# Row remainders of two batches stored in one transfer, and the last output tile stored in two column halves

## The chip, the cores and the metric

The kernel runs on one core of one Trainium2 chip. The metric is the device time of one execution in microseconds. Three runs of the kernel before the change took 370.40, 368.73 and 370.27 us, so their median is 370.27 us.

## The reference

Eight batches of twelve heads go through attention whose denominator has one extra term, and the result, laid side by side by head as rows of 768 numbers, goes through a gated long convolution along the 448 positions of a batch and a last projection:

```python
scores = scale * np.matmul(q, k.transpose(0, 1, 3, 2))
m = np.max(scores, axis=-1, keepdims=True)
e = np.exp(scores - m)
attn = e / (np.sum(e, axis=-1, keepdims=True) + np.exp(-m) + 1e-09)
x = np.matmul(attn, v)                      # then heads side by side: B, S, 768
x1, x2, x3 = split(x @ w_proj, 3)           # each B, S, 768
x2_conv = irfft(rfft(x2, axis=1) * rfft(filter_fft, axis=0), axis=1)
return (x1 * x2_conv * x3) @ w_out          # out: 8, 448, 768, float32
```

The inputs q, k and v are 8 x 12 x 448 x 64, and the output is 8 x 448 x 768 in float32.

## The kernel before

Every piece of work is a task with an engine, a cost, tokens that it needs and makes, and buffers that it takes and gives back (`add`, L82). A planner (`Plan.run`, L90) walks the tasks in the order of a table, `plan.ORDER` (L433), with one number for each task, and writes each engine's instructions in the order that it finds. So the order is fixed when the program is built. Each engine works through its own list in order, and an instruction that waits holds up everything behind it on its engine.

Attention is worked by pairs of heads, six pairs to a batch and 48 in all. For the later batches SP (SyncE) loads q, k and v, POOL (GpSimd) casts them, and SP issues transposing transfers into `qT` (L628) and `kT` (L635) before TensorE makes the scores (L867, L869). The dense part of a batch follows: folds of the rows, a projection (L1096), for batches 3 to 7 a transposing transfer of that projection (L1113, tile `x2`, called `x` in the profile) and then the spectrum on TensorE (L1145), gates (L1197), the inverse transform and the gated product.

The output projection (`output`, L1009 and L1010) makes tiles of 128 rows and 384 columns in PSUM. A batch has 448 rows, that is three tiles of 128 rows (`st` 0 to 2) and a rest of 64. The rests of an even batch and of the odd one behind it share one tile (`st` 3 of the odd batch): partitions 0 to 63 hold the even batch's rest, 64 to 127 the odd one's. ScalarE copies each PSUM tile to half of the columns of an `osb` tile of 128 x 768 floats (`project_back`, L1319); three such buffers rotate. When both column halves (`ch` 0 and 1) are there, SP stores the tile (`store`): with one transfer for `st` 0 to 2 (L1326), with two for the shared rest tile, one to each batch (L1328 and L1329). So each row stored is 3,072 bytes long.

The last batch's tasks marked `keep` are written out at the very end, behind a branch to a slower, numerically safe version that is not taken here (L1540 is the tail behind it). There the tiles come in the order `st` 0, 1, 3, 2; three of the eight projections are made before the branch.

Of the kernel before, what the change touches and what calls it, by code (L numbers as in the profile page):

```python
# [18 lines left out]
B, H, S, DH = 8, 12, 448, 64  # L19
D = H * DH  # L20
SP = 112
# [4 lines left out]
DCH = 384  # L26
# [4 lines left out]
REM = S - 3 * 128  # L31
# [10 lines left out]
class Plan:  # L42
# [39 lines left out]
    def add(self, eng, cost, want, emit, need=(), make=(), take=(), give=(), dma=0.0, run=256, n=1, after=0.0, begun=(), late=0.0, turn=False, part=None, keep=False, port=False, rows=128):  # L82
        want = self.ORDER[len(self.tasks)] if self.ORDER else want + self.SHIFT.get(part, 0.0)
        if eng == "SP":
            dma *= self.STRETCH
        if eng == "DVE" and port:
            cost += self.SHARED
        self.tasks.append((want, len(self.tasks), eng, cost, emit, need, make, take, give, dma, after, run, n, begun, late, turn, keep, port or eng == "POOL" and not dma, rows))
# [227 lines left out]
def kernel(  # L316
# [11 lines left out]
    nc = tc.nc  # L328
# [105 lines left out]
    add = plan.add  # L434
# [583 lines left out]
    def dense(b, calm=True):  # L1018

        L = {}  # L1020
# [37 lines left out]
        for ds in (slice(0, 3), slice(3, 6)) if b else (slice(0, 3), slice(3, 4), slice(4, 6)):  # L1058
            g, m = ds.start, (ds.stop - ds.start) / 3
            slow = 0.3 + 0.7 * m  # L1060
            w = DENSE[b] - 2.5 - (0.4 if g else FOLD[b]) if b else FOLD0[(g + 1) // 2]
# [253 lines left out]
        def project_back(st, ch):  # L1315
            n = 128 if st < 3 or b % 2 else REM
            if ("os", st) not in L:
                L["os", st] = otp.tile([128, D], F32, name="osb")
            nc.scalar.copy(  # L1319
                L["os", st][:n, ch * DCH : (ch + 1) * DCH], L["O", st, ch][:n, :DCH]  # L1320
            )

        def store(st):
            osb = L["os", st]
            if st < 3:
                nc.sync.dma_start(out[b, st * 128 : (st + 1) * 128, :], osb)  # L1326
                return
            for i in range(1 + b % 2):  # L1328
                nc.sync.dma_start(out[b - b % 2 + i, 384:S, :], osb[i * REM : (i + 1) * REM])  # L1329

        def O(st, ch):
            keep = b + 1 == n_batches
            last = keep and (st, ch) not in TAIL
            hy, os_ = ("ho" if last else "hy", ("O", b, st, ch)), ("os", (b, st))
            if keep and not last:
                plan.open.append((st, ch))
            w = span(0.97, OUT[b])
            need = [("y", b, 0)] if st < 3 else [("y", b - b % 2, 1), ("y", b, 1)]
            mem_ = ("yT", b) if st < 3 else ("yR", b // 2)
            if 2 * st + ch < 3:  # L1340

                add("PE", 0.65, w, lambda: project(st, ch, 0, hy), need=[("y", b, 0, 0), ("y", b, 0, 1), "wout", ("G", b)],
                    make=[("O4", b, st, ch)], take=[hy])
                add("PE", 0.33, w + 1.5, lambda: project(st, ch, 1, hy), need=[("y", b, 0, 2), ("O4", b, st, ch)],
                    make=[("O", b, st, ch)], give=[mem_], keep=last)
            else:
                add("PE", 0.98, w, lambda: project(st, ch, None, hy), need=need + ["wout"], make=[("O", b, st, ch)],
                    take=[hy], give=[mem_], keep=last)
            add("ACT", 0.38, w, lambda: project_back(st, ch), need=[("O", b, st, ch)], make=[("os", b, st)],
                take=[os_], give=[hy], keep=keep)  # L1350
            if ch == 1:
                add("SP", 0.62, w, lambda: store(st), need=[("os", b, st)], make=[("store", b, st)], give=[os_], dma=0.87 if st < 3 else 1.1, run=180, keep=keep)
# [239 lines left out]
```

## Time and profile before

| | |
|---|---|
| median of three runs | 370.27 us (368.73 to 370.40) |
| time of the profiled execution | 369.05 us |
| its span, first to last instruction | 367.3 us |
| time around the span | 1.75 us |
| ScalarE copies of L1319 | 56, of 489 ns |
| stores of whole tiles (L1326) | 24, 384 KB each, landing 3.6 us after issue (median) |
| stores of rests (L1329) | 8, 192 KB each, landing 3.5 us after issue (median) |
| moved by DMA | 68.41 MB in 132,019 packets |

PE is TensorE, PEld its weight loads, DVE is VectorE, ACT is ScalarE, and a "q" behind an engine's name (SPq) marks its sequencer, which issues transfers. The DMA share is the mean busy share of the core's 16 DMA engines; it can read a little over 1, since packets of several transfers overlap. "Landing" is the time from the start of a transfer's issue to the signal that all its data has arrived.

### The profile page before, as it was taken

What the parts mean: (1) busy time and instruction counts of PE and PEld (TensorE: products, weight loads), DVE (VectorE), ACT (ScalarE), POOL (GpSimd) and SP (SyncE); (2) the same over time, 40 slices, a digit from 0 to 9 for tenths busy, and PEclk for the clock granted to TensorE, in tenths of its full rate; (3) what the DMA queues carried; (4) which work ended last, traced back from release to release, by engine and by line L of the source; (5) the groups of instructions that cost most, each with busy time, mean ns of one, the idle gap of its engine ahead of it and who ended that gap; (6) DMA issues with size and microseconds to landing.
All of it is one profiled execution on the core that took longest, in us unless ns stands there. A gap on an engine that the chain in (4) does not pass through costs nothing. (4 is left out here: it accounts for less than half of the span.)

```text
span 367.3 us, 9351 instructions
## 1 busy us (share of the span) xinstructions
PE 358.3 (98%) x3612; PEld 215.1 (59%) x3612; DVE 259.6 (71%) x671; ACT 262.0 (71%) x453; POOL 112.0 (30%) x247
## 2 busy tenths in 40 slices
PE   7999999999999999999999999999999999999995
PEld 6666665656655665654564555665555556565653
DVE  6678297984998587882787767783478848767570
ACT  5987886768777868876787766888688794464523
POOL 7680563243551444515226343321200000000000
PEclk9999999999999999999999999999999999999999
DMA  8999999979998999898999999899942066163125
GB/s 206 277 240 222 251 214 216 216 168 220 192 235 225 237 283 244 214 230 206 212 219 233 283 188 217 217 215 236 219 83 45 2 87 130 43 102 114 44 93 173
DMA packets 132019, 68.41 MB, mean 186 GB/s; under 512 B 88765, under 2 KB 128384, under 8 KB 131968
## 3 DMA queue, kind: packets, MB, share of 16 engines
q1 hardware_dynamic: 127248, 62.11, 75.1%
q0 software_dynamic: 4480, 5.41, 8.6%
q8 instruction: 29, 0.48, 0.5%
q10 hardware_dynamic: 240, 0.23, 0.3%
q14 instruction: 22, 0.18, 0.2%
HBM read 43.86 MB, written 11.01 MB: 149 GB/s over the span
## 5 line engine op out<-in xcount | busy, mean ns | idle before, releaser
L880 ACT ACTIVATE e<-psum 128x896 bf16<-128x896 f32 x138 | 122.1, 922 | 27.2 <-PE psum L867 25.5
L1197 PE MATMUL psum<-xT,wproj_bf 128*128 128x448 bf16 x576 | 121.6, 352 | 0.6 <-ACT cr L1253 0.6
L1197 PEld LDWEIGHTS <-wproj_bf 128*128 128x128 bf16 x576 | 53.9, 98 | 48.7 <-issue 5.4
L1010 PE MATMUL psum<-wout_bf,yT 128*128 128x384 bf16 x288 | 53.8, 326 | 0.0
L906 PE MATMUL psum<-vn,e 128*128 128x65 bf16 x1104 | 44.3, 194 | 0.0
L906 PEld LDWEIGHTS <-e 128*128 128x128 bf16 x1104 | 39.4, 98 | 6.5 <-issue 2.8
L867 PE MATMUL psum<-qT,kT 64*128 64x448 bf16 x288 | 42.1, 354 | 0.1
L1157 ACT CAST xs<-psum 113x384 bf16<-113x384 f32 (+1 forms) x64 | 29.2, 486 | 17.2 <-PE psum L1145 10.4
L664 POOL CAST nat<-nat 112x512 bf16<-112x512 f32 x36 | 23.5, 661 | 58.8 <-DMA nat<-in_q_dram 58.6
L1319 ACT COPY osb<-psum 128x384 f32<-128x384 f32 x56 | 25.7, 489 | 18.5 <-PE psum L1010 11.7
L1010 PEld LDWEIGHTS <-yT 128*128 128x128 bf16 x288 | 27.4, 98 | 18.0 <-issue 0.6
L1163 DVE TENSOR_TENSOR t<-xs,hrs 113x768 bf16<-113x768 bf16 (+1 forms) x64 | 36.5, 594 | 1.7 <-ACT xs L1157 1.6
L1096 PE MATMUL psum<-xf,wproj_bf 128*128 128x456 bf16 x180 | 37.5, 356 | 0.0
L921 DVE TENSOR_TENSOR xb<-psum,den 128x512 bf16<-128x512 f32 x48 | 33.2, 691 | 1.7
L1213 DVE TENSOR_TENSOR g<-x,psum 128x448 bf16<-128x448 bf16 x42 | 25.8, 616 | 10.2 <-PE psum L1197 7.5
L1253 ACT CAST cr<-psum 128x452 bf16<-128x452 f32 x48 | 24.7, 549 | 8.4 <-PE psum L1244 7.0
L1211 ACT CAST x<-psum 128x448 bf16<-128x448 f32 x42 | 22.3, 541 | 10.9 <-PE psum L1197 10.5
L684 POOL CAST nat<-nat 128x384 bf16<-128x384 f32 x29 | 16.3, 569 | 39.6 <-DMA nat<-in_k_dram 35.6
L886 ACT ACTIVATE er<-psum 128x448 bf16<-128x448 f32 x46 | 25.2, 557 | 4.2 <-PE psum L869 4.2
L1074 PE MATMUL psum<-wproj_bf,xf 128*113 128x384 bf16 x144 | 27.1, 328 | 0.0
L1096 PEld LDWEIGHTS <-wproj_bf 128*128 128x128 bf16 x180 | 17.0, 98 | 16.3 <-issue 1.5
L696 POOL CAST vn<-nat 128x192 bf16<-128x192 f32 x58 | 21.5, 401 | 16.2 <-DMA nat<-in_v_dram 15.6
(136 smaller groups left out, 477.1 us busy)
## 6 DMA issues: line engine op xcount, KB each, us to landing
nat<-in_q_dram SPq DMA_DIRECT2D x47, 224.0 KB, 4.4
out_dram<-osb SPq DMA_DIRECT2D x24, 384.0 KB, 3.6
nat<-in_k_dram SPq DMA_DIRECT2D x41, 192.0 KB, 4.8
nat<-in_v_dram SPq DMA_DIRECT2D x41, 192.0 KB, 4.5
wproj_bf<-in_moe_w_proj_dram POOLq DMA_DIRECT2D x2, 1152.0 KB, 12.2
rests<-in_k_dram SPq DMA_DIRECT2D x8, 192.0 KB, 4.5
rests<-in_v_dram SPq DMA_DIRECT2D x8, 192.0 KB, 5.0
out_dram<-osb SPq DMA_DIRECT2D x8, 192.0 KB, 3.5
```

The lines of the kernel that those rows point to most:

```text
L867: nc.tensor.matmul(sc[:, u, 0:S], kT[b % 2][c, hp, t, :], qT[b % 2][c, hp, :])
L880: nc.scalar.activation(to, of, AF.Exp, scale=SCALE)
L906: nc.tensor.matmul(out_bank(u)[:, n, :], P["e"][1 + t][:, u * S + n * 128 : u * S + n * 128 + 128], vn[b % 2][:, hp, 4 * u + t, :], start= ...
L921: nc.vector.tensor_tensor(W["xb", b][:, hp].rearrange("p n (u d) -> p u n d", u=2), op[:, :, :, 0:DH], rec[:].unsqueeze(3).to_broadcast([1 ...
L1010: nc.tensor.matmul(ops[:n, :DCH], y[:, dt, 0:n], wout_bf[:, dt, ch * DCH : (ch + 1) * DCH], start=(dt == 0), stop=(dt == NDT - 1),)
L1074: nc.tensor.matmul(pps[:FQ, :DCH], W["xf", b][:, kt, pg, 0:FQ], wproj_bf[:, kt, D + ch * DCH : D + (ch + 1) * DCH], start=(kt == 0), stop= ...
L1096: nc.tensor.matmul(pps, wproj_bf[:, kt, D + dt * 128 : D + (dt + 1) * 128], W["xf", b][:, kt], start=(kt == 0), stop=(kt == NDT - 1),)
L1157: nc.scalar.copy(L["xs", par, ch][:K, pg % 2, :], L["Z", pg, ch][:K, :DCH])
L1163: nc.vector.tensor_tensor(t[:K], L["xs", par, ch][:K], h, op=ALU.mult)
L1197: nc.tensor.matmul(p[:, :S], wproj_bf[:, kt, 2 * part * D + dt * 128 : 2 * part * D + (dt + 1) * 128], xT()[:, kt, 0:S], start=(kt == 0), ...
L1213: nc.vector.tensor_tensor(g[:, dt, :], L["x1", dt], p[:, :S], op=ALU.mult)
L1319: nc.scalar.copy(L["os", st][:n, ch * DCH : (ch + 1) * DCH], L["O", st, ch][:n, :DCH])
```

## The change

The two stores of a rest tile become one transfer, from all 128 partitions to a destination of two batches by 64 rows by 768 columns. In the last batch the tile `st` 2, which is the last to be projected, is stored in two transfers of 384 columns, each as soon as ScalarE has copied that half. `plan.ORDER` has one number more for the added task, and two numbers around it differ; everything else in the table is as it was.

```diff
-        def store(st):
-            osb = L["os", st]
+        def store(st, chs=slice(0, 2)):
+            osb, c = L["os", st], slice(chs.start * DCH, chs.stop * DCH)
             if st < 3:
-                nc.sync.dma_start(out[b, st * 128 : (st + 1) * 128, :], osb)
+                nc.sync.dma_start(out[b, st * 128 : (st + 1) * 128, c], osb[:, c])
                 return
-            for i in range(1 + b % 2):
-                nc.sync.dma_start(out[b - b % 2 + i, 384:S, :], osb[i * REM : (i + 1) * REM])
+            nc.sync.dma_start(out[b - 1 : b + 1, 384:S, :], osb)
...
-            add("ACT", 0.38, w, lambda: project_back(st, ch), need=[("O", b, st, ch)], make=[("os", b, st)],
+            add("ACT", 0.38, w, lambda: project_back(st, ch), need=[("O", b, st, ch)], make=[("os", b, st), ("os", b, st, ch)],
                 take=[os_], give=[hy], keep=keep)
-            if ch == 1:
+            if keep and st == 2:
+                add("SP", 0.45, w, lambda: store(st, slice(ch, ch + 1)), need=[("os", b, st, ch)], make=[("store", b, st, ch)], give=[os_], dma=0.45, run=180, keep=keep)
+            elif ch == 1:
                 add("SP", 0.62, w, lambda: store(st), need=[("os", b, st)], make=[("store", b, st)], give=[os_], dma=0.87 if st < 3 else 1.1, run=180, keep=keep)
```

On TensorE, ScalarE, VectorE and GpSimd the instructions stand in the same order as before; only the names of some buffers are counted differently. SP's order changes at the stores alone. The first place is the store of the rest tile of batches 0 and 1, in the middle of the program (the trace has it at 161.8 us). Ahead of it and behind it stand loads, a transposing transfer into `kT` and one into `x`. Before:

```order
L658 DMA nat<-in_q_dram 112x2x256
L1329 DMA out_dram<-osb 64x768 x2
L658 DMA nat<-in_q_dram 112x2x256
L679 DMA ks<-in_v_dram 128x2x192
L658 DMA nat<-in_q_dram 112x2x256
L635 DMA_TRANSPOSE kT_90<-nat 128x12x128
L1113 DMA_TRANSPOSE x_2985<-xb 128x12x128
```

The same place after the change:

```order
L658 DMA nat<-in_q_dram 112x2x256
L1328 DMA out_dram<-osb 2x64x768
L658 DMA nat<-in_q_dram 112x2x256
L679 DMA ks<-in_v_dram 128x2x192
L658 DMA nat<-in_q_dram 112x2x256
L635 DMA_TRANSPOSE kT_90<-nat 128x12x128
L1113 DMA_TRANSPOSE x_2984<-xb 128x12x128
```

Two transfers of 64 rows have become one whose destination has three dimensions, 2 by 64 by 768; nothing else moved. The rest tiles of batches 2 and 3, 4 and 5, and 6 and 7 change in the same way, the last of them in the second place. That place is the end of SP's list, behind the branch (L1540), where the last batch's four tiles are stored. Before:

```order
L1540 UNCONDITIONAL_BRANCH x2
L1326 DMA out_dram<-osb 128x768
L1329 DMA out_dram<-osb 64x768 x2
L1326 DMA out_dram<-osb 128x768 x2
L1587 UNCONDITIONAL_BRANCH
```

The same place after the change:

```order
L1541 UNCONDITIONAL_BRANCH x2
L1326 DMA out_dram<-osb 128x768
L1328 DMA out_dram<-osb 2x64x768
L1326 DMA out_dram<-osb 128x768
L1326 DMA out_dram<-osb 128x384 x2
L1588 UNCONDITIONAL_BRANCH
```

The pair of 64 rows is one transfer there too, and the last of the two whole tiles has become two of 384 columns. There are five transfers as before.

More of the change, by code (lines that the diff above doesn't have):

```diff
@@ new lines @@
+    plan.ORDER = (2, 0, 1, 152, 3, 4, 0, 0, 2, 1, 3, 4, 2, 9, 32, 0, 1, 6, 0, 5, 7, 9, 10, 10, 4, 11, 4, 12, 2, 3, 8, 9, 2, 5, 3, 6, 8, 12, 6, 14, 13, 5, 8, 4, 7, 11, 17, 12, 16, 15, 10, 13, 6, 14, 13, 23, 22, 20, 19, 14, 18, 15, 16, 17, 26, 30, 24, 23, 12, 19, 16, 20, 21, 29, 34, 25, 26, 30, 25, 37, 18, 25, 20, 19, 28, 24, 27, 36, 52, 32, 29, 31, 43, 23, 31, 22, 30, 69, 49, 44, 36, 48, 27, 33, 26, 35, 86, 58, 57, 37, 46, 24, 38, 29, 39, 90, 59, 60, 34, 51, 28, 41, 33, 40, 97, 64, 65, 39, 52, 35, 45, 32, 42, 116, 78, 80, 38, 53, 49, 54, 59, 41, 53, 44, 42, 55, 46, 43, 56, 45, 57, 51, 40, 50, 49, 58, 63, 47, 58, 55, 48, 60, 59, 60, 65, 50, 61, 63, 54, 62, 61, 69, 71, 57, 64, 68, 64, 66, 71, 66, 67, 62, 68, 77, 67, 70, 75, 65, 69, 73, 76, 74, 77, 76, 72, 72, 88, 79, 78, 87, 70, 75, 74, 73, 80, 80, 83, 82, 82, 81, 78, 79, 84, 83, 85, 85, 104, 86, 84, 101, 94, 93, 99, 90, 93, 86, 95, 87, 98, 89, 90, 88, 97, 96, 106, 89, 101, 97, 111, 107, 98, 122, 109, 99, 121, 100, 91, 103, 92, 102, 94, 105, 95, 116, 102, 113, 100, 117, 103, 118, 104, 135, 120, 105, 137, 110, 107, 123, 114, 112, 106, 119, 110, 127, 115, 125, 112, 128, 113, 129, 150, 120, 121, 130, 139, 118, 156, 126, 109, 144, 124, 108, 141, 124, 131, 116, 142, 123, 143, 128, 134, 117, 132, 119, 149, 127, 175, 130, 122, 158, 136, 126, 157, 132, 146, 129, 138, 125, 160, 139, 147, 131, 148, 133, 155, 169, 140, 135, 154, 162, 138, 198, 154, 136, 184, 161, 141, 170, 147, 164, 144, 159, 134, 172, 148, 163, 137, 166, 142, 177, 151, 207, 178, 149, 190, 173, 153, 179, 156, 165, 143, 167, 145, 189, 159, 171, 146, 192, 160, 194, 211, 163, 164, 173, 196, 165, 214, 186, 157, 202, 181, 158, 203, 169, 174, 155, 176, 150, 200, 167, 197, 162, 191, 168, 213, 172, 223, 205, 170, 209, 193, 161, 216, 175, 185, 166, 212, 176, 219, 174, 206, 171, 220, 177, 74, 22, 34, 15, 21, 44, 47, 3, 7, 11, 17, 1, 11, 34, 32, 78, 48, 64, 42, 61, 34, 63, 36, 58, 33, 54, 30, 76, 47, 55, 31, 9, 9, 5, 5, 7, 6, 8, 7, 17, 18, 18, 29, 22, 10, 8, 13, 11, 14, 16, 10, 15, 12, 27, 25, 21, 35, 27, 21, 15, 19, 13, 20, 23, 14, 24, 16, 37, 39, 28, 45, 30, 33, 20, 26, 17, 28, 32, 18, 31, 19, 42, 44, 29, 56, 36, 36, 21, 38, 22, 41, 40, 23, 46, 25, 51, 53, 33, 65, 37, 43, 24, 47, 26, 48, 50, 27, 49, 28, 57, 60, 59, 37, 42, 68, 39, 81, 51, 62, 35, 66, 38, 67, 40, 91, 93, 61, 83, 56, 74, 44, 75, 45, 88, 89, 57, 100, 102, 69, 109, 67, 96, 61, 98, 99, 63, 104, 64, 114, 115, 77, 52, 101, 62, 106, 66, 107, 65, 112, 113, 69, 120, 122, 82, 125, 75, 117, 73, 127, 118, 77, 128, 76, 143, 144, 100, 145, 87, 129, 78, 140, 82, 141, 139, 84, 152, 153, 108, 133, 56, 155, 91, 149, 88, 150, 151, 89, 157, 92, 172, 171, 125, 162, 94, 160, 93, 161, 95, 170, 169, 102, 179, 180, 129, 182, 107, 177, 104, 178, 176, 105, 184, 110, 196, 195, 137, 81, 197, 117, 185, 109, 186, 112, 193, 194, 116, 205, 204, 142, 210, 124, 201, 120, 202, 203, 123, 215, 130, 222, 224, 157, 213, 129, 216, 132, 217, 131, 220, 221, 133, 233, 230, 165, 199, 92, 247, 148, 236, 142, 237, 229, 143, 238, 144, 257, 256, 186, 240, 147, 242, 146, 243, 149, 253, 255, 154, 266, 268, 192, 264, 163, 254, 155, 261, 260, 160, 262, 159, 275, 276, 198, 115, 279, 167, 272, 165, 273, 164, 280, 271, 168, 292, 291, 211, 299, 183, 287, 173, 296, 286, 181, 297, 184, 312, 309, 229, 308, 192, 298, 182, 305, 190, 306, 307, 189, 316, 317, 230, 253, 133, 327, 203, 313, 193, 322, 314, 199, 323, 198, 334, 335, 247, 326, 201, 324, 202, 331, 206, 332, 333, 205, 342, 341, 254, 345, 211, 338, 209, 340, 339, 208, 349, 215, 360, 357, 260, 152, 343, 213, 350, 216, 351, 217, 356, 355, 221, 369, 370, 264, 358, 220, 367, 227, 368, 366, 226, 374, 231, 388, 387, 278, 372, 230, 375, 229, 384, 238, 385, 386, 237, 398, 397, 287, 357, 168, 391, 241, 393, 242, 394, 395, 244, 407, 252, 418, 421, 304, 396, 243, 408, 256, 414, 259, 415, 413, 257, 429, 428, 314, 420, 261, 424, 264, 426, 425, 265, 431, 268, 443, 446, 323, 195, 430, 269, 432, 267, 436, 271, 437, 438, 272, 450, 457, 332, 454, 280, 448, 277, 464, 449, 288, 465, 296, 480, 482, 351, 467, 289, 466, 292, 477, 298, 479, 478, 299, 490, 489, 358, 403, 204, 483, 301, 488, 305, 494, 487, 309, 495, 310, 504, 505, 371, 497, 312, 496, 311, 501, 314, 502, 503, 313, 513, 512, 376, 514, 320, 509, 317, 510, 511, 318, 518, 325, 529, 530, 382, 221, 521, 326, 519, 324, 520, 323, 526, 528, 329, 537, 539, 385, 541, 335, 527, 330, 532, 533, 331, 534, 336, 559, 557, 398, 553, 344, 546, 342, 547, 340, 551, 550, 343, 565, 566, 402, 416, 224, 558, 349, 562, 353, 564, 563, 352, 568, 355, 585, 586, 424, 573, 357, 569, 354, 570, 356, 577, 576, 361, 593, 592, 430, 581, 366, 588, 369, 589, 590, 370, 596, 374, 603, 604, 442, 226, 594, 372, 597, 373, 598, 377, 602, 601, 376, 612, 613, 444, 614, 382, 607, 381, 608, 609, 380, 616, 385, 627, 628, 452, 610, 383, 617, 386, 619, 387, 620, 625, 388, 624, 631, 632, 453, 478, 228, 31, 38, 40, 35, 46, 39, 41, 43, 45, 50, 52, 51, 47, 54, 48, 53, 56, 55, 84, 52, 80, 53, 82, 50, 85, 54, 108, 73, 111, 76, 105, 71, 103, 67, 87, 55, 92, 58, 62, 70, 68, 72, 121, 71, 119, 70, 86, 90, 81, 85, 71, 72, 41, 131, 136, 93, 95, 60, 94, 59, 66, 75, 63, 79, 70, 79, 49, 123, 72, 110, 68, 83, 89, 84, 87, 132, 133, 92, 73, 43, 134, 79, 130, 91, 135, 80, 94, 95, 96, 98, 99, 107, 77, 46, 142, 83, 126, 88, 137, 81, 101, 102, 103, 104, 106, 114, 124, 74, 146, 85, 138, 97, 154, 90, 110, 109, 112, 111, 113, 117, 147, 86, 148, 105, 159, 165, 96, 158, 163, 103, 91, 156, 164, 97, 167, 100, 96, 166, 98, 168, 99, 114, 115, 116, 120, 118, 124, 119, 121, 123, 122, 128, 131, 130, 173, 101, 174, 127, 183, 108, 175, 126, 181, 106, 190, 134, 192, 114, 189, 113, 187, 111, 138, 139, 135, 136, 188, 132, 191, 115, 198, 118, 141, 146, 140, 148, 200, 119, 208, 144, 206, 122, 207, 121, 143, 145, 147, 153, 211, 127, 199, 125, 212, 128, 149, 151, 150, 152, 214, 163, 209, 126, 223, 134, 218, 154, 225, 135, 159, 158, 162, 160, 167, 164, 227, 137, 232, 139, 219, 161, 226, 136, 168, 166, 169, 170, 172, 188, 235, 145, 228, 138, 241, 174, 234, 141, 173, 175, 176, 177, 179, 183, 231, 140, 239, 178, 244, 251, 152, 245, 250, 151, 108, 246, 249, 156, 252, 153, 111, 294, 178, 295, 180, 153, 301, 185, 290, 179, 140, 155, 156, 181, 171, 187, 180, 182, 184, 185, 189, 194, 191, 248, 150, 269, 193, 259, 158, 270, 195, 258, 157, 263, 190, 285, 172, 265, 162, 267, 161, 202, 203, 196, 200, 281, 201, 277, 169, 278, 166, 204, 207, 206, 210, 282, 174, 274, 197, 289, 175, 293, 177, 214, 216, 212, 213, 288, 176, 284, 170, 283, 171, 205, 209, 208, 215, 300, 218, 310, 191, 302, 186, 311, 228, 303, 187, 221, 223, 226, 225, 227, 236, 304, 188, 315, 194, 321, 234, 318, 195, 232, 231, 233, 235, 239, 255, 325, 200, 319, 197, 329, 242, 320, 196, 237, 240, 244, 249, 250, 257, 328, 204, 330, 245, 336, 344, 210, 383, 389, 240, 188, 381, 390, 239, 400, 249, 180, 399, 248, 406, 255, 182, 217, 238, 220, 219, 224, 222, 241, 251, 252, 243, 246, 248, 348, 214, 346, 256, 347, 212, 145, 337, 207, 362, 261, 353, 258, 354, 219, 359, 259, 151, 352, 218, 373, 228, 364, 224, 267, 276, 268, 274, 371, 266, 361, 222, 363, 223, 262, 263, 265, 270, 365, 225, 380, 234, 382, 236, 279, 281, 280, 284, 378, 232, 377, 233, 275, 286, 277, 282, 404, 247, 376, 269, 401, 245, 290, 289, 291, 293, 303, 307, 379, 235, 409, 254, 392, 283, 410, 253, 305, 302, 308, 306, 315, 317, 403, 250, 402, 246, 412, 298, 417, 258, 310, 309, 313, 311, 316, 320, 405, 251, 411, 294, 447, 456, 281, 470, 473, 295, 201, 462, 463, 287, 459, 286, 199, 468, 290, 486, 304, 208, 491, 306, 493, 308, 210, 271, 292, 288, 272, 285, 273, 295, 296, 297, 299, 300, 301, 423, 266, 427, 312, 422, 263, 183, 416, 262, 440, 322, 433, 319, 435, 270, 434, 318, 187, 419, 260, 444, 275, 442, 274, 325, 330, 326, 329, 439, 321, 441, 273, 445, 276, 324, 328, 327, 331, 451, 278, 460, 284, 461, 285, 336, 342, 338, 339, 452, 279, 455, 282, 334, 337, 335, 340, 472, 294, 453, 333, 471, 293, 347, 345, 352, 348, 355, 362, 458, 283, 476, 297, 474, 346, 481, 300, 354, 356, 360, 361, 364, 378, 469, 291, 484, 303, 475, 349, 492, 307, 363, 365, 367, 368, 369, 379, 485, 302, 498, 366, 500, 507, 316, 499, 506, 315, 215, 515, 516, 321, 517, 322, 218, 583, 367, 554, 345, 229, 341, 344, 359, 343, 350, 353, 370, 374, 373, 372, 375, 377, 522, 327, 524, 380, 523, 328, 217, 525, 381, 535, 332, 536, 384, 222, 508, 319, 545, 339, 542, 337, 396, 404, 388, 399, 531, 383, 560, 350, 556, 346, 408, 410, 405, 409, 538, 333, 540, 334, 392, 395, 386, 389, 548, 341, 552, 348, 555, 347, 400, 412, 401, 406, 549, 393, 543, 338, 579, 362, 544, 390, 575, 360, 419, 420, 421, 422, 435, 425, 561, 351, 584, 368, 567, 411, 582, 364, 429, 431, 432, 433, 438, 440, 572, 358, 578, 363, 574, 414, 591, 371, 434, 437, 441, 439, 443, 447, 571, 359, 587, 428, 622, 636, 396, 606, 611, 384, 230, 647, 651, 405, 660, 412, 232, 644, 401, 639, 395, 234, 643, 404, 662, 415, 235, 387, 391, 394, 397, 413, 407, 415, 418, 417, 423, 426, 427, 600, 378, 595, 436, 605, 379, 225, 618, 446, 599, 375, 615, 445, 227, 580, 365, 630, 391, 626, 392, 457, 473, 456, 464, 623, 450, 634, 393, 645, 402, 472, 481, 477, 482, 621, 389, 629, 390, 454, 458, 455, 459, 640, 398, 641, 397, 638, 400, 475, 476, 479, 480, 637, 465, 635, 394, 654, 408, 633, 460, 653, 407, 485, 484, 488, 489, 492, 495, 642, 399, 659, 411, 646, 474, 657, 410, 490, 491, 494, 496, 499, 498, 663, 417, 656, 413, 668, 501, 661, 414, 500, 497, 509, 507, 510, 517, 666, 418, 671, 506, 683, 687, 430, 682, 685, 431, 236, 675, 681, 428, 691, 438, 238, 688, 433, 693, 437, 237, 448, 462, 461, 449, 451, 467, 463, 469, 466, 468, 471, 470, 648, 403, 650, 483, 652, 406, 231, 649, 487, 655, 409, 658, 493, 233, 669, 422, 664, 416, 665, 419, 503, 513, 502, 511, 680, 519, 672, 423, 674, 425, 515, 524, 516, 525, 670, 420, 667, 421, 504, 514, 505, 508, 676, 426, 679, 427, 673, 424, 520, 521, 522, 523, 677, 518, 684, 429, 690, 435, 696, 536, 689, 434, 527, 526, 528, 529, 533, 539, 686, 432, 692, 436, 697, 534, 694, 439, 531, 530, 532, 535, 540, 546, 699, 442, 695, 440, 701, 541, 698, 441, 538, 537, 544, 542, 545, 547, 700, 443, 702, 543, 704, 708, 444, 705, 707, 445, 239, 703, 706, 446, 711, 449, 241, 709, 447, 710, 448, 240, 712, 450, 242, 713, 451, 243, 1, 486, 678, 512)
```

1 line of the change is left out of this document (removed).

## Prediction

> **What bounds the kernel now.** I read the page first, for the engine that has no idle time.
>
> ```profile
> PE 358.3 (98%) x3612; PEld 215.1 (59%) x3612; DVE 259.6 (71%) x671; ACT 262.0 (71%) x453; POOL 112.0 (30%) x247
> DMA  8999999979998999898999999899942066163125
> ```
>
> TensorE (PE) is busy for 358.3 of 367.3 us. The DMA engines are full too, at 8 or 9 tenths up to slice 29 (some 270 us), and mostly idle after that. The waits of PE come next:
>
> ```profile
> PE psum L869 <- DVE xb L921: 0.6, 1, 0.6
> PE psum L1197 <- ACT cr L1253: 0.6, 1, 0.6
> ```
>
> No wait of PE in that view is for a transfer. PE hardly lacks data at present, so a store that gets shorter in the middle of the program gives PE nothing, while one that gets longer may push back the loads and transposes behind it until PE waits. At the end it is the reverse: the chain that ended last is PE's last projections, one copy, and then a store.
>
> ```profile
> 358.06 5.05 PE psum L1010 x30
> 363.11 0.02 issue
> 363.13 0.48 ACT osb L1319
> ```
>
> The copy ends at 363.61 and the span at 367.3 us; the 3.7 us between them are a transfer and its end. SP's timeline, the last store's own rows and the windows of the DMA engines (the last two numbers are the DMA share and GB/s) show what happens there:
>
> ```profile
> 358.97 0.33 SPq L1326 DMA_DIRECT2D out_dram<-osb  x1
> 360.71 1.14 SPq L1329 DMA_DIRECT2D out_dram<-osb  x2
> 361.94 2.03 SPq L1326 DMA_DIRECT2D out_dram<-osb  x2
> ...
> L1326 SPq DMA_DIRECT2D out_dram<-osb x1: 338/338/338, 363.6 to 363.6; - x1
> DMA to landing us min/median/max: 2.7/2.7/2.7
> ```
>
> ```profile
> 359.80:360.80 1.00, 1.00 (x8) 0.59 (x6) 0.00 (x0) 0.48 (x1) 0.00 (x0) 1.00 0.98 387
> 361.80:362.80 1.00, 1.00 (x8) 0.58 (x6) 0.00 (x0) 0.48 (x1) 0.00 (x0) 1.00 0.94 197
> 364.00:365.50 1.50, 0.00 (x0) 0.00 (x0) 0.00 (x0) 0.00 (x0) 0.00 (x0) 1.00 0.99 391
> 361.50:362.00 0.50, 0.50 (x5) 0.31 (x4) 0.00 (x0) 0.16 (x1) 0.00 (x0) 1.00 0.31 74
> 365.50:366.00 0.50, 0.00 (x0) 0.00 (x0) 0.00 (x0) 0.00 (x0) 0.00 (x0) 1.00 0.30 117
> 366.00:366.50 0.50, 0.00 (x0) 0.00 (x0) 0.00 (x0) 0.00 (x0) 0.00 (x0) 1.00 0.00 0
> ```
>
> A whole tile of 128 rows fills all 16 engines at 387 to 391 GB/s; the pair of 64 rows fills them as well (0.94), but moves 197 GB/s. So the pair takes 393 KB / (197 / 0.94 = 210 GB/s) = 1.9 us where a whole tile takes 1.0 us. One engine at work moves 391 / 0.99 / 16 = 24.7 GB/s, so **one row of 3,072 bytes occupies one engine for 0.124 us**.
>
> **Part 1: the rest tile in one transfer.** It removes four issues and four transfers and adds none. What it costs depends on how many of the 16 engines share the new transfer, and this trace has no such shape. All that SP transfers now has an outermost count that 16 divides: 128 partitions, 112 or 64. The new destination counts 2 outermost, then 64 rows, then 768 columns. The two ends are: all 16 engines, 128 x 0.124 / 16 = 1.0 us, which saves 0.9 us per pair; or rows dealt out by the outermost count that both sides share, hence 2 engines with 64 rows each, 64 x 0.124 = 7.96 us, which costs 7.96 - 1.9 = **6.1 us** more on those two. I take the second end: every transfer that is seen to fill the engines has a count to be dealt out evenly to 16, and this one has not.
>
> The Trainium skill, "DMA: Bandwidth & Descriptors", section "Why a DMA increments its semaphore by 16 and not by 1", says it outright: the engines used are the largest number up to 16 that divides the slowest dimension, other than 1, of both sides; by that rule the new transfer gets 2 engines and the sum is the slow one. The same page's rules for kernel authors advise one transfer of 128 partitions in place of two halves, by which this part would save 0.9 us. No run here shows either so far.
>
> *At the tail*, on two engines: the pair's data begins at 362.00 - 0.31 x 0.5 = 361.85 us, and I let the new transfer, issued at the same 360.71, begin there too. It ends at 361.85 + 7.96 = 369.81. Each store behind it needs its share from those two engines: 8 rows of the whole tile (1.0 us), and 8 half rows of each column half (0.5 us each), so the last data moves at 371.8 us. Now the last data lies just short of 366.0 (the row after it is empty), the landing at 363.64 + 2.7 = 366.3 and the end at 367.3. The same 0.3 and 1.0 us behind 371.8 give 373.1: **+5.8 us**.
>
> *In the middle*, three rest tiles go out, at 161.8, 248.9 and 331.3. Behind the third SP has nothing to issue for 13 us, which hides it:
>
> ```profile
> 331.29 1.26 SPq L1329 DMA_DIRECT2D out_dram<-osb  x2
> 344.91 0.35 SPq L1326 DMA_DIRECT2D out_dram<-osb  x1
> ```
>
> Behind the other two stand transfers that PE needs, above all the transposes of L1113 into x. First their issue on SP's timeline, then the landing of the two pairs, and then that of the two transposes:
>
> ```profile
> 169.33 1.43 SPq L1113 DMA_TRANSPOSE x<-xb  x1
> 257.30 1.29 SPq L1113 DMA_TRANSPOSE x<-nat  x1
> ```
>
> ```profile
> L1329 SPq DMA_DIRECT2D out_dram<-osb x2: 565/723/881, 161.8 to 162.4; - x2
> DMA to landing us min/median/max: 3.6/3.7/3.7
> L1329 SPq DMA_DIRECT2D out_dram<-osb x2: 583/707/831, 248.9 to 249.7; - x2
> DMA to landing us min/median/max: 3.7/3.9/4.1
> ```
>
> ```profile
> DMA to landing us min/median/max: 3.7/3.7/3.7
> DMA to landing us min/median/max: 4.1/4.1/4.1
> ```
>
> Then PE's first uses of those two tiles, what the weight loads of that line waited for, and the windows between:
>
> ```profile
> 175.39 0.34 PE L1145 MATMUL psum<-x,ft 113*112 113x384 bf16 x1
> 263.37 0.35 PE L1145 MATMUL psum<-x,ft 113*112 113x384 bf16 x1
>   DMA x<-xb: 0.2, 1
> ```
>
> ```profile
> 165.00:170.00 5.00, 5.00 (x30) 2.28 (x29) 1.91 (x5) 3.52 (x7) 4.78 (x13) 1.00 0.76 192
> 170.00:175.00 5.00, 5.00 (x45) 2.55 (x44) 0.63 (x1) 3.64 (x7) 0.20 (x1) 1.00 0.98 217
> 258.00:263.00 5.00, 5.00 (x64) 2.78 (x59) 1.91 (x5) 3.20 (x4) 0.00 (x0) 1.00 1.00 248
> ```
>
> One such transpose has no slack at all already (0.2 us of waiting). The first pair lands at 162.4 + 3.6 = 166.0, and x at 169.33 + 3.7 = 173.0, which leaves 2.4 us before PE's use at 175.39. If the transfers run 6.1 us late and win back at most the idle shares on the way (0.24 x 4 us + 0.02 x 3 us = 1.0 us), PE waits up to 6.1 - 1.0 - 2.4 = 2.7 us. At the second place x lands at 257.30 + 4.1 = 261.4, 2.0 us early; with no idle share PE waits up to 6.1 - 2.0 = 4.1 us. Both are upper ends, since shares with overlapping packets hide some slack; the lower ends are 0. I take half of each, 1.4 and 2.0 us, and do not add them: PE that is already late has that much more room at the second place. So **+2.0 us**, and it carries through to the tail, as nothing behind it leaves PE idle. The merged store also keeps its `osb` buffer 6.1 us longer; three rotate, so ScalarE meets it again two tiles later:
>
> ```profile
> L1319 ACT COPY osb<-psum x5: 484/497/498, 188.2 to 200.0; 128x384 f32<-128x384 f32 x5
> ```
>
> Behind the first pair that is at 188 us at the earliest, long after 166.0 + 6.1 = 172.1, so it costs nothing.
>
> **Part 2: column halves.** One transfer is added, none is waited for by an engine, and 8 half rows per engine cost the same in sum as 8 whole ones. The first half leaves at the end of the copy that starts at 362.20 rather than 363.13, but both queue behind the rest tile on the two engines, so it gains nothing in my case. If a half row costs as much as a whole one, it adds 1.0 us; if the halves overlap with less, at most 0.5 us is won. I take 0.
>
> **Sum.** 5.8 + 2.0 = +7.8 us on the profiled execution: 369.05 + 7.8 = 376.9. That execution lies 1.2 us under the median of the three runs; the four executions shown average 369.6, so I name 369.6 + 7.8 = **377.4 us**.
>
> **Rivals.**
>
> *All 16 engines share the new transfer* (the change does what its words say). Then the rest tile takes 1.0 us from 361.85, the whole tile follows to 363.9, the first half to 364.4, and the second, issued at 363.64, begins 0.85 us later (358.97 to 359.82 for the store that found the engines idle) and ends at 365.0 instead of 366.0. That is 0.9 to 1.0 us faster, about 368.7, which is within 0.5% of no change (0.5% is about what a measurement of this kernel can tell from none). PE in the middle gains nothing, for it hardly waits for a transfer. For it: the 64-row stores do use all 16. Against it: the outermost 2. It decides where the merged store takes under about 2 us. Chance 0.15, and 0.03 for something more that makes it faster by over 0.5%.
>
> *Two engines, but the slack covers the middle*: the lower ends above, 369.6 + 5.8 = 375.4. For it: PE waits for no transfer now, and the transfers are issued when SP's other waits allow. Chance 0.20.
>
> *Two engines, and the middle is starved*: both upper ends add, as SP issues late what PE makes late, 2.7 + 4.1 + 5.8 = 12.6, about 382.2. For it: the DMA engines are full up to 270 us and have little to catch up with. Chance 0.10.
>
> **How the numbers follow.** My forecast has 0.52, the two on its side 0.20 and 0.10, full spread 0.18 in all. The range reaches from 373.5 (tail alone over the lowest run, 368.73 + 5.8, less 1.0 for a half store or a start that comes earlier) to 382.5, and leaves out the full spread. Slower by over 0.5%: 0.52 + 0.20 + 0.10 = 0.82; within 0.5%: 0.15; faster: 0.03.
>
> **What would show it.** In the profile after: four merged stores that land some 10 us after issue instead of 3.6; in the windows from 362 to 370 us a DMA share near 2/16 = 0.13 and about 50 GB/s; a span that ends 9 to 10 us after the last copy instead of 3.7; PE waiting at L1145 for a transposed x near 175 and 263 us, by 1 to 3 us each. I would be wrong if the merged store lands in 3 us or less at 390 GB/s, and wrong in size if PE's last matmul ends at 363.1 as now.

## The result, and the profile after

| | before | after |
|---|---|---|
| median of 5 runs, us | 370.27 (368.14 to 370.80) | 387.57 (386.25 to 387.93) |
| ratio, 95% interval | | 1.0493 (1.0466 to 1.0519) |
| profiled execution, us | 369.05 | 387.93 |
| its span, us | 367.3 | 386.1 |
| mean granted clock of TensorE | 1.000 | 0.978 |

The change costs 17.3 us where 7.8 were forecast: the direction was right, and the time lies outside the range. The two spans differ by 18.8 us. The chain that ended last splits that in two. It still ends in PE's last projections and this copy of L1319 (start, duration, what):

```profile
375.22 0.48 ACT osb L1319
```

The last copy starts at 375.22 instead of 363.13, so PE comes **12.1 us** later to its end. The copy ends at 375.70 and the span at 386.1: 10.4 us lie behind it where there were 3.7, and that is the tail, **6.7 us** more. First the tail. SP's timeline, and then a window behind the last copy (the last three numbers are PE's granted clock, the DMA share and GB/s):

```profile
372.80 0.61 SPq L1328 DMA_DIRECT2D out_dram<-osb  x1
373.77 3.14 SPq L1326 DMA_DIRECT2D out_dram<-osb  x3
```

```profile
380.00:384.00 4.00, 0.00 (x0) 0.00 (x0) 0.00 (x0) 0.00 (x0) 0.00 (x0) 0.50 0.13 51
```

No compute engine works from 380 to 384 us, and the transfers move 51 GB/s at a share of 0.13, which is 2 / 16. Two engines are at work and fourteen have nothing to do. The rule of the Trainium skill that the prediction cited ("DMA: Bandwidth & Descriptors", "Why a DMA increments its semaphore by 16 and not by 1") gives 2 engines for an outermost 2; this trace agrees, with 0.13.

Now PE's 12.1 us. Its longest waits (in total, times, longest, in us):

```profile
PE psum L1145 <- DMA x<-xb: 4.9, 1, 4.9
PE psum L1145 <- DMA x<-nat: 3.9, 1, 3.9
```

Before, no wait of PE in this view was for a transfer. Now it waits 8.8 us in all for two transposed `x` tiles at L1145, near 176 and 270 us. What lies ahead of the first of them is on SP's timeline:

```profile
163.54 0.69 SPq L1328 DMA_DIRECT2D out_dram<-osb  x1
...
168.42 6.94 SPq L635 DMA_TRANSPOSE kT<-nat  x1
175.47 2.23 SPq L1113 DMA_TRANSPOSE x<-xb  x1
```

The same stretch before, in the same view:

```profile
167.34 1.49 SPq L635 DMA_TRANSPOSE kT<-nat  x1
169.33 1.43 SPq L1113 DMA_TRANSPOSE x<-xb  x1
```

The issue of the transposing transfer into `kT` takes 6.94 us instead of 1.49. SP works through one list, so the issue of `x` stands behind it and comes at 175.47 instead of 169.33. The engines moved less meanwhile. Here are windows of after, and one of before:

```profile
170.00:172.00 2.00, 2.00 (x13) 1.01 (x11) 0.00 (x0) 2.00 (x4) 0.00 (x0) 1.00 3.45 111
172.00:174.00 2.00, 2.00 (x29) 1.03 (x28) 0.63 (x1) 1.04 (x3) 0.00 (x0) 1.00 0.13 35
177.00:180.00 3.00, 0.00 (x0) 0.00 (x0) 0.22 (x1) 0.00 (x0) 1.29 (x5) 0.66 1.19 159
182.00:184.00 2.00, 2.00 (x7) 0.91 (x6) 0.33 (x1) 0.07 (x1) 0.11 (x1) 0.50 1.30 241
274.00:276.00 2.00, 1.93 (x16) 1.41 (x17) 0.53 (x3) 0.79 (x2) 0.40 (x1) 0.50 1.10 349
```

```profile
172.00:174.00 2.00, 2.00 (x29) 1.07 (x28) 0.54 (x1) 0.71 (x2) 0.00 (x0) 1.00 0.94 213
```

From 172 to 174 us the share is 0.13 where it was 0.94: two engines work off the store and their part of the transfers behind it, the other fourteen have run dry, and SP, which could feed them, is held in one instruction. The 3.45 of the first row can't be read as engines at work: behind a transposing transfer the share goes far above 1 here, and to 4.56 in a window of the kernel before that is shown further down. There the bytes are the measure, 111 GB/s where the same two microseconds had 199 before. The three rows below these show what follows. PE is idle from 177 to 180 us, and its granted clock falls from 1.00 to 0.50. It is still 0.50 at 182 to 184, when PE works again, and back at 1.00 from 186 to 188; the second wait repeats the 0.50 (at 274 to 276). PE's timeline shows what half the clock costs (three groups behind the first wait, one behind the second):

```profile
180.76 0.57 PE L1145 MATMUL psum<-x,ft 113*112 113x384 bf16 x1 [4.88 <-DMA x<-xb]
181.12 2.45 PE L1197 MATMUL psum<-xT,wproj_bf 128*128 128x448 bf16 x6
...
186.98 1.30 PE L1197 MATMUL psum<-xT,wproj_bf 128*128 128x448 bf16 x6
279.57 2.44 PE L1197 MATMUL psum<-xT,wproj_bf 128*128 128x448 bf16 x12
```

Two of these groups in the kernel before:

```profile
179.62 1.30 PE L1197 MATMUL psum<-xT,wproj_bf 128*128 128x448 bf16 x6
267.48 2.44 PE L1197 MATMUL psum<-xT,wproj_bf 128*128 128x448 bf16 x12
```

Six matmuls of L1197 take 2.45 us behind the wait and 1.30 us later. The starts give the whole account. PE is 0.5 us late when it is ready for the first tile (175.88 for 175.39), 5.4 when it has it (180.76), and 7.4 at the group of 186.98 (179.62 before): the half clock cost 2.0. It is 6.8 late when it is ready for the second tile (270.12 for 263.37), 10.7 when it has it (274.07), and 12.1 at the group of 279.57 (267.48 before): 1.4 more. So the 12.1 us are **8.8 of waiting and 3.4 of half clock**, since the 0.5 ahead of the first wait and the 0.6 won back between the two cancel. The prediction had no term for the clock.

### The profile page after: what moved, and what is told of

Read it like the earlier page. It is cut to its first block, busy times and chain, and to the rows that moved or that the text cites. A ratio compares the mean times of both kernels' runs of the same rounds, so it can differ in the third digit from the quotient of the medians.

```text
span 386.1 us, 9346 instructions
## 1 busy us (share of the span) xinstructions
PE 361.0 (93%) x3612; PEld 215.9 (56%) x3612; DVE 261.0 (68%) x671; ACT 262.3 (68%) x453; POOL 113.6 (29%) x247
## 5 line engine op out<-in xcount | busy, mean ns | idle before, releaser
L1197 PE MATMUL psum<-xT,wproj_bf 128*128 128x448 bf16 x576 | 123.5, 357 | 0.0
L1197 PEld LDWEIGHTS <-wproj_bf 128*128 128x128 bf16 x576 | 54.6, 99 | 49.0 <-issue 6.4
L664 POOL CAST nat<-nat 112x512 bf16<-112x512 f32 x36 | 24.3, 682 | 63.8 <-DMA nat<-in_q_dram 63.7
L1163 DVE TENSOR_TENSOR t<-xs,hrs 113x768 bf16<-113x768 bf16 (+1 forms) x64 | 38.2, 621 | 3.2 <-ACT xs L1157 3.0
L1319 ACT COPY osb<-psum 128x384 f32<-128x384 f32 x56 | 25.7, 489 | 18.5 <-PE psum L1010 11.7
L919 DVE TENSOR_SCALAR den<-psum 128x8 f32<-128x8 f32 x48 | 7.9, 164 | 27.3 <-PE psum L906 25.7
```

Source lines behind the costliest of these rows:

```text
L1163: nc.vector.tensor_tensor(t[:K], L["xs", par, ch][:K], h, op=ALU.mult)
L1197: nc.tensor.matmul(p[:, :S], wproj_bf[:, kt, 2 * part * D + dt * 128 : 2 * part * D + (dt + 1) * 128], xT()[:, kt, 0:S], start=(kt == 0), ...
L1319: nc.scalar.copy(L["os", st][:n, ch * DCH : (ch + 1) * DCH], L["O", st, ch][:n, :DCH])
```

## The experiments

The questions were: whether the outermost count is the cause; what each of the four merged stores costs, and whether the costs add; what the column halves do; what the clock takes; and by what path the middle is late.

**The rest tile interleaved.** The kernel before, with the rests of two batches on alternate partitions (row r of the even batch on 2r, of the odd one on 2r + 1), so that one transfer goes to a destination that counts 64, then 2, then 768:

```diff
-                o = REM * (b % 2)
-                y, c = W["yR", b // 2][:, ds, o : o + REM], slice(384, S)
+                y, c = W["yR", b // 2][:, ds, b % 2 :: 2], slice(384, S)
...
-            for i in range(1 + b % 2):
-                nc.sync.dma_start(out[b - b % 2 + i, 384:S, :], osb[i * REM : (i + 1) * REM])
+            nc.sync.dma_start(out[b - 1 : b + 1, 384:S, :].rearrange("b r d -> r b d"), osb)
```

> The kernel before, with the rests of two batches interleaved over the partitions (row r of the even batch on partition 2r, of the odd one on 2r+1), so that one transfer stores both and its destination counts 64 outermost, then 2, then 768; no column halves. Theory A (the outermost count, which both sides must share, sets how many engines take part): 64 is dealt out to all 16, the merged store lands 2.5 to 4 us after issue, PE never waits for x, and the time is 0 to 0.5 us below the kernel before. Rival B (a store with three dimensions, or to two places of the output far apart, is slow however it is counted): merged stores land some 10 us after issue again and the time is about 387 us.

Measured: 368.82 us against 369.40 for the kernel before, ratio 0.9999 (0.9968 to 1.0030). The landing of the last merged store (issued at 359.64), and the window in which most of its data moves:

```profile
L1327 SPq DMA_DIRECT2D out_dram<-osb x1: 592/592/592, 359.6 to 359.6; - x1
...
DMA to landing us min/median/max: 2.7/2.7/2.7
```

```profile
361.00:362.00 1.00, 1.00 (x7) 0.39 (x4) 0.00 (x0) 0.48 (x1) 0.00 (x0) 1.00 1.01 393
```

One transfer with three dimensions to two places of the output lands after 2.7 us, and all 16 engines are at work at 393 GB/s. So neither that it is one transfer nor its three dimensions cost anything; the order of its counts does.

**Rows cut at 62.** The kernel before, with each of the two stores of batches 4 and 5 cut in 62 and 2 rows. They stay plain two-dimensional transfers, and nobody waits for them there:

```diff
+            cuts = (0, 62, 64) if b == 5 else (0, 64)
             for i in range(1 + b % 2):
+                for lo, hi in zip(cuts, cuts[1:]):
-                nc.sync.dma_start(out[b - b % 2 + i, 384:S, :], osb[i * REM : (i + 1) * REM])
+                    nc.sync.dma_start(out[b - b % 2 + i, 384 + lo : 384 + hi, :], osb[i * REM + lo : i * REM + hi])
```

> The kernel before, with the third pair of rest stores (331 us, hidden) cut into 62 and 2 rows each, so four transfers. If the engines that take part are the largest number up to 16 that divides the outermost count, 62 rows go to 2 engines, 31 rows each: 31 x 0.124 = 3.8 us, and the first 62-row store lands about 5.2 us after issue, the second 4 us after it. Rival (rows are dealt out one by one to all 16): both land 3.0 to 3.5 us after issue, as the 64-row stores there do. The time is that of the kernel before in both cases.

Measured: one run of 369.73 us, beside 368.84 for the kernel before. The trace gives no landing for these transfers, so the expectation's 5.2 us can't be compared. The windows show the engines:

```profile
334.00:335.00 1.00, 1.00 (x7) 0.62 (x6) 0.44 (x2) 1.00 (x3) 0.00 (x0) 1.00 0.13 31
338.00:339.00 1.00, 1.00 (x7) 0.47 (x6) 0.54 (x4) 0.23 (x1) 0.00 (x0) 1.00 0.13 52
```

The share is 0.13 again, at 31 to 52 GB/s in these two, and between 0.10 and 0.14 in every window from 334 to 343 us, where the kernel before has next to nothing from 335 on. The two stores of 2 rows are too short for that (one row for each of two engines, 0.12 us by the price of a row), so the 62 rows run on two engines. 62 is large, and 2 is the largest number up to 16 that divides it. So it is the divisor that counts, not the size of the outermost count.

**One merged store at a time.** Four kernels, each the kernel before with one of the four rest tiles merged as in the change (7 in this line stands for the last pair, 1, 3 and 5 for the others):

```diff
+            if b == 7:
+                nc.sync.dma_start(out[b - 1 : b + 1, 384:S, :], osb)
+                return
             for i in range(1 + b % 2):
```

The last pair, at the tail:

> The kernel before, with only the last of the four rest tiles (batches 6 and 7) stored in one transfer. Theory A: nothing changes up to the last copy; then the merged store and the two whole tiles behind it queue on two engines, and the span ends 10 us after the last copy instead of 3.7: 6 to 7 us above the kernel before, about 376 us. Rival: PE's waits make all of the loss; then no change.

The first pair:

> The kernel before, with only the first rest tile (batches 0 and 1, at 162 us) stored in one transfer. Theory A: PE waits about 5 us for x at 176 us and then runs at half clock for some 4 us of work: 6.5 to 7 us above the kernel before, about 376 us. Rival (the first wait is caught up later, since DMA idles after 280 us and PE has slack): 3 us or less above.

The second pair:

> The kernel before, with only the second rest tile (batches 2 and 3, at 249 us) stored in one transfer. If the waits add up as they did in the changed kernel: PE waits about 4 us for x near 263 us, with 1.5 us for the clock behind it: 5 to 5.5 us above the kernel before, about 375 us. The prediction's reading (half of 4.1 us): 2 us above. Rival: the wait there was only there because PE was late already; then no change.

The third pair:

> The kernel before, with only the third rest tile (batches 4 and 5, at 331 us) stored in one transfer, which nothing on SP follows for 13 us. Theory A: the merged store lands some 10 us after issue, and the time is that of the kernel before within 0.5 us. Rival (a merged store costs its 6 us wherever it stands): about 375 us.

| merged alone | median, us (before: 368.88) | ratio, 95% interval |
|---|---|---|
| batches 0, 1 | 373.52 | 1.0128 (1.0083 to 1.0172) |
| batches 2, 3 | 375.77 | 1.0169 (1.0127 to 1.0211) |
| batches 4, 5 | 369.30 | 1.0015 (0.9990 to 1.0039) |
| batches 6, 7 | 375.68 | 1.0180 (1.0144 to 1.0215) |

The four excesses add up to 0.0128 + 0.0169 + 0.0015 + 0.0180 = 0.0492, and the whole change has 0.0493. The half widths of the four intervals, combined as independent errors, leave 0.0075 of room, 2.8 us, so it is luck that the two agree to 0.0001. Within that room **the costs add, and the column halves are worth nothing measurable beside them**. With the last pair alone, the chain ends in this copy, and the span at 374.0 us:

```profile
363.22 0.48 ACT osb L1319
```

PE is where it was (363.13 before), and the span ends 6.7 us later (367.3 before): the tail costs that by itself. With the first pair alone, the wait and SP's timeline read:

```profile
PE psum L1145 <- DMA x<-xb: 3.4, 1, 3.4
```

```profile
167.86 6.09 SPq L635 DMA_TRANSPOSE kT<-nat  x1
```

Up to this wait SP's list is that of the changed kernel, and yet the wait is 3.4 us here and 4.9 there: a profile is one execution, and a single wait can differ by 1.5 us between two.

With the second pair alone (stored at 250.00 us), the wait, SP's timeline and two windows:

```profile
PE psum L1145 <- DMA x<-nat: 3.6, 1, 3.6
```

```profile
251.22 4.80 SPq L679 DMA_DIRECT2D ks<-in_v_dram  x1
...
262.38 2.13 SPq L1113 DMA_TRANSPOSE x<-nat  x1
```

```profile
254.00:256.00 2.00, 2.00 (x11) 1.01 (x12) 0.00 (x0) 1.91 (x3) 0.00 (x0) 1.00 0.13 49
270.00:274.00 4.00, 4.00 (x13) 1.63 (x12) 2.72 (x5) 2.69 (x5) 2.67 (x6) 0.51 1.13 225
```

The picture is the same at both places: a merged store, an issue of some 5 to 6 us on SP a few instructions later, a stretch in which two engines work alone (0.13), and PE's wait. The instruction that is held is not of one kind: a transposing transfer at the first place, a load of `v` at the second. And `x` is issued at 262.38 where it was 257.30. Behind the wait the clock is at 0.51 for 4 us.

**The column halves alone.** The change, with the rest tile in two transfers as before:

```diff
-            nc.sync.dma_start(out[b - 1 : b + 1, 384:S, :], osb)
+            for i in range(1 + b % 2):
+                nc.sync.dma_start(out[b - b % 2 + i, 384:S, :], osb[i * REM : (i + 1) * REM])
```

> The changed kernel with the rest tiles stored by two transfers of 64 rows again, so that only the column halves of the last tile are new. Theory A: the loss is all in the merged stores, so the time is that of the kernel before within 0.5 us (the pair and the whole tile still keep the engines busy until 364.7 us, and the halves follow). Rival: the added transfer or its 1,536-byte rows cost something by themselves; then 1 us or more above the kernel before.

Measured: 369.57 us against 369.40, ratio 1.0000 (0.9976 to 1.0024).

**Interleaved, with the halves.** The change, with the interleaving of the first experiment:

> The changed kernel (column halves kept) with the interleaved rests of e6. Theory A: 0.5 to 1.0 us below the kernel before, since after the last copy only half a tile is left and nothing queues ahead of it: the span ends 2.8 to 3.2 us after the last copy instead of 3.7. Rival B: about 387 us. A second rival (two half-width stores cost as much as two whole ones): no faster than e6.

Measured: 368.49 us against 369.40, ratio 0.9987 (0.9969 to 1.0005). Its last copy starts at 362.71 and its span ends at 366.2, that is 3.0 us behind the copy's end where the kernel before has 3.7. It has the lowest median of all that were run, but its interval holds 1, so it can't be told from the kernel before.

**PE kept busy in the two waits.** The change, with 80 and 62 matmuls of the zero tile `idle` ahead of the two spectra that wait. What they write is overwritten by the spectrum behind them:

```diff
+            if calm and (b, pg, ch) in ((3, 2, 0), (5, 2, 0)):
+                for _ in range({3: 80, 5: 62}[b]):
+                    nc.tensor.matmul(xps[:, 0:128], idle, idle)
```

> The changed kernel, with 80 small matmuls of zeros on TensorE ahead of the first spectrum of batch 3 and 62 ahead of that of batch 5, that is in the two places where PE waits 4.9 and 3.9 us for a transposed x; their output is overwritten. Theory A (a wait lets the granted clock fall to 0.5 for the time after it, which costs 2.0 and 1.5 us more): the clock stays at 1.00 there and the time is 3 to 4 us below the changed kernel, about 384 us. Rival: the clock fell for another reason, or the wait itself is all that is lost; the time stays at 387.5 us or rises.

Measured: 383.89 us, ratio 1.0410 (1.0380 to 1.0439) to the kernel before, where the change alone has 1.0493. PE's timeline and the page's clock:

```profile
176.05 4.63 PE L1146 MATMUL psum<-idle 128*128 128x128 bf16 x80
180.51 0.33 PE L1148 MATMUL psum<-x,ft 113*112 113x384 bf16 x1
180.68 1.30 PE L1200 MATMUL psum<-xT,wproj_bf 128*128 128x448 bf16 x6
267.69 3.63 PE L1146 MATMUL psum<-idle 128*128 128x128 bf16 x62
271.16 0.33 PE L1148 MATMUL psum<-x,ft 113*112 113x384 bf16 x1
```

```profile
PEclk9999999999999999999999999999999999999996
```

The spectrum starts at 180.51, hardly earlier than the 180.76 of the change, so the transfer is as late as it was. But the six matmuls behind it take 1.30 us, and the clock stays up to the end of PE's work. The last copy of this kernel, in its chain, starts at 370.89 instead of 375.22:

```profile
370.89 0.48 ACT osb L1322
```

By the medians **3.7 us of the change's 17.3 come back** (3.1 by the ratios), and by the last copies of the two profiled executions 4.3. Not all of it is the clock's. PE gets its tiles here 4.5 us (180.51 - 176.05) and 3.5 us (271.16 - 267.69) after its work ahead of them, against 4.9 and 3.9 in the change, and these 0.9 us are not shown to be the clock's. 4.3 - 0.9 leaves **3.4 us for the clock**, as PE's starts gave above.

**The merged stores from another queue.** The change, with the first three merged stores issued by ScalarE instead of SP:

```diff
-            nc.sync.dma_start(out[b - 1 : b + 1, 384:S, :], osb)
+            (nc.sync if b == 7 else nc.scalar).dma_start(out[b - 1 : b + 1, 384:S, :], osb)
```

> The changed kernel, with the first three merged stores issued from ScalarE's queue instead of SP's (the one at the end stays on SP). Theory A1 (the middle loses because SP's own issue is held while its transfers queue behind the merged store on two engines): the issues behind 162 and 250 us take their usual 0.3 to 1.5 us again, two queues share those two engines, x comes less late, and the time falls by 5 us or more, to 382 us or less. A2 (whatever shares those two engines is late by the 6 us, by whichever queue it comes): about 387 us as in the changed kernel. The end of the program is the same in both, 6.5 us above the kernel before.

Measured: 384.74 us, ratio 1.0444 (1.0420 to 1.0468), so 2.8 us less than the change by the medians and 1.8 by the ratios, with intervals that just touch. PE's waits, and the timelines of SP and of ScalarE's queue (ACTq) put together:

```profile
PE psum L1145 <- DMA x<-nat: 3.5, 1, 3.5
PE psum L1145 <- DMA x<-xb: 2.6, 1, 2.6
```

```profile
160.27 1.12 ACTq L1328 DMA_DIRECT2D out_dram<-osb  x1
169.90 2.23 SPq L635 DMA_TRANSPOSE kT<-nat  x1
172.23 2.43 SPq L1113 DMA_TRANSPOSE x<-xb  x1
252.32 0.54 ACTq L1328 DMA_DIRECT2D out_dram<-osb  x1
255.36 7.54 SPq L628 DMA_TRANSPOSE qT<-nat  x1
```

At the first place SP is held for less (2.23 us in place of 6.94), `x` is issued at 172.23 instead of 175.47, and the wait falls from 4.9 to 2.6 us. But the store also goes out 3.3 us earlier there, at 160.27 instead of 163.54, and the share leaves 0.13 at 169 us (0.49 from 169 to 170), so by the prediction's 8 us and by the share its data are over when `kT` is issued. So the gain at this place can be the earlier start as well as the other queue. At the second place the store is on ScalarE's queue too, and SP's issue of `qT` 3 us behind it still takes 7.54 us, and PE still waits 3.5. SP is held there with no merged store in its own queue, so theory A1 fails as it stands. The time lies between what the two theories wanted. How much of the middle is SP's held issue and how much is the sharing of the two engines stays open.

## Why the prediction was wrong in size

**Two engines, 64 rows each.** Right. The share is 2 / 16 at the tail, the interleaved store takes the cost away, and the cut at 62 rows brings the two engines back without a third dimension. Alone at the third place (issued at 331.6), the merged store's data moves until 342.1, 10.5 us behind its issue, which fits the prediction's "some 10 us". The 0.9 us a pair that a merged store would save on all 16 engines are not seen, but not excluded: interleaved, the interval is 0.9968 to 1.0030, which is 1.1 us to either side.

**Tail, +5.8 us.** Right, and 0.9 us too small: 6.7 in the change, and 6.7 with that store alone. In the change the share falls to nothing at 384.6, 8.9 us behind the last copy's end where the sum had 8.2 (371.8 - 363.61), and the span ends 1.5 us later where the sum had 1.3. So 0.7 of the 0.9 us lie in the time that the two engines work; why they need it no run tells.

**The third rest tile, hidden.** Right: 1.0015 with an interval that holds 1.

**The column halves, 0.** Right: 1.0000 in their own kernel.

**Middle, +2.0 us.** Here it failed. PE's end moved by 12.1 us, 8.8 of waiting and 3.4 of half clock, in three ways that the step had excluded or left out:

- *"I take half of each, 1.4 and 2.0 us, and do not add them: PE that is already late has that much more room at the second place."* The waits are 4.9 and 3.9 us, and they add. The second is 3.6 us when the first pair is left as it was, so the lateness of PE gave no room at all. A reason that fits, argued and not tested: the second merged store and the transfers behind it follow from what PE makes, so they are late with it. In the trace that store is issued 6.4 us late (255.25 for 248.86), and PE is 6.8 us late when it needs the tile.
- *The upper end of the first wait, 2.7 us, was no bound.* It let the transfers run 6.1 us late and win 1.0 back. In the trace `x` is used at 180.76 where it landed at 173.0, 7.7 us later. Of these 1.1 us were there when `kT` was issued (168.42 for 167.34), 5.1 more had come when `x` was issued (175.47 for 169.33), and the transfer itself took up to 5.3 us in place of 3.7. PE came 0.5 us later (its work ahead of the wait ends at 175.88) and had 2.4 us of slack: 7.7 - 0.5 - 2.4 = 4.8, the wait measured. The step had thought of two engines that are late, and not of SP, which was held in an issue and let the other fourteen run dry. That the held issue delays `x` is in the trace; that it alone makes the wait is not shown. The 2.7 was too low for the store alone as well, where the wait is 3.4.
- *The clock had no term.* It costs 2.0 us behind the first wait and 1.4 behind the second, 3.4 of the 12.1; with PE kept busy the clock stays up, and that much comes back beside the shorter waits.

The rival *"two engines, and the middle is starved"* had the right sign for each piece: both waits, added, SP issuing late what PE makes late. At 382.2 it lacked 0.9 us at the tail, 2.0 us of waits (8.8 for 6.8), and 3.4 us of the clock: together 6.3, and its 12.6 became 18.8.

## What to carry to other kernels

Before two transfers are merged, look at the outermost count of both sides of the new one. Here 64 and 128 ran on all 16 engines, 2 and 62 on two, and a merged store on two moved its data until 10.5 us behind its issue where the two that it replaced landed after 3.3. Interleaving the rows, so that a multiple of 16 stands outermost, gave the same single transfer at full width. A long narrow transfer is not hidden because other engines are free: an issue of SP's behind it was held, and with it all that stood behind that, even where the narrow transfer came from another queue. It cost nothing measurable where SP had nothing to issue behind it. And a wait of PE of 3 to 5 us is dearer than it looks, since the clock falls with it.

## What the runs showed of the hardware that was not expected

**An issue is held while most engines are idle.** Before, SP's two longest issues of one transfer behind 160 us take 3.29 and 4.39 us (one of the first loads, at 20.8 us, takes 4.63). Two windows of before from the end of the longest, a transposing transfer into `xT` at L973 (224.30 to 228.69):

```profile
227.00:227.50 0.50, 0.50 (x6) 0.26 (x6) 0.49 (x2) 0.50 (x2) 0.00 (x0) 1.00 4.56 100
228.00:228.70 0.70, 0.70 (x6) 0.41 (x5) 0.67 (x3) 0.70 (x2) 0.00 (x0) 1.00 0.08 18
```

The share goes to 4.56 at 100 GB/s and then to 0.08, while the issue lasts on. So even without a merged store an issue can last while the engines idle. What is new is the length at these places: behind a merged store issues take 6.94 and 6.06 us in the change, and 6.09 and 4.80 with one pair alone, where the same issues before take 1.49, 0.47, 1.49 and 0.54. The view doesn't show what the issue waits for. That it waits for room on the two full engines is what one would think, and no run singles it out.

**The clock follows PE's waits.** In the change PE is idle from 175.88 to 180.76. Its clock is at 0.66 on the mean from 177 to 180, which is 1 us at full and 2 us at half, so it falls at 178.0, 2.1 us into the wait. It is back when PE has worked for 4 us:

```profile
184.00:186.00 2.00, 2.00 (x19) 0.86 (x17) 1.83 (x3) 1.05 (x3) 2.00 (x4) 0.80 1.10 208
```

A mean of 0.80 over 2 us is 0.8 us at half, hence 184.8. The second wait, from 270.12 to 274.07, gives other times:

```profile
272.00:274.00 2.00, 0.00 (x0) 0.00 (x0) 0.00 (x0) 0.00 (x0) 0.00 (x0) 0.89 0.93 268
276.00:278.00 2.00, 2.00 (x10) 0.92 (x8) 1.97 (x4) 1.96 (x5) 2.00 (x6) 0.76 1.21 256
```

By the same working the clock falls at 273.6, 3.4 us into the wait, and is back at 277.0, after 2.9 us of work. The Trainium skill, "TensorE: Matmul & The Clock Gate", section "Part 1: The HAM clock gate (the "warmup" mystery)", has the clock halve after an idle window of about 3.4 us and return after about as long at work. The trace agrees with the half and, at 4.0 and 2.9 us, roughly with the return. At the second wait it agrees with the fall; at the first the fall came after 2.1 us of idle time already.
